# The a * b product in one piece: attention's steps and the group's issued only between products of 18 matmuls

## The chip, the cores and the metric

The kernel runs on one core of a Trainium2 chip. The time is that of one execution on the device, in microseconds. Shown for the kernel before are three runs: 725.28 us in the median, 724.61 to 728.33. TensorE (PE, and PEld for its weight loads) multiplies into PSUM, a memory of eight banks per partition; VectorE (DVE) and ScalarE (ACT) copy out of PSUM and compute element by element; GpSimd (POOL) does so in SBUF alone; SyncE (SP) issues the DMAs.

## The reference

Three layers follow one another. Attention has a sigmoid in place of the softmax; its 4 batches of 448 tokens with 12 heads of 64 make 1792 tokens of 768 values.

```python
scores = scale * np.matmul(q, k.transpose(0, 1, 3, 2)) - np.log(S)
attn_out = np.matmul(1.0 / (1.0 + np.exp(-scores)), v)
x = tokens(attn_out)                       # 1792 x 768
x = ((x @ w_a) * (x @ w_b)) @ w_out        # d_ff = 1536
logits = x @ phi                           # 8 experts x 4 slots
d = softmax over the tokens; slot_input = d.T @ x
slot_out = relu(slot_input @ w1) @ w2      # per expert
out = softmax over the slots of logits @ slot_out
```

## The kernel before, in words

The product with `w_out` is never made token by token: `w_out` is multiplied with `phi` once (`wphi`), which gives the logits from g = a * b, and the slots take their sums from g as well.

The middle of the kernel is the loop over four batches. In it, `ab` goes through the 12 chunks of 128 columns of d_ff. A chunk has two products, a (i = 0) and b (i = 1); each is 18 full matmuls of 128x128 weights with 448 columns into one "ab" PSUM buffer: weights and x are split into a high and a low part, and s = 0, 1, 2 are high*high, high*low and low*high over six pieces (L492). Behind a, ScalarE copies the result (L501), behind b, VectorE multiplies it in (L504): g^T, one of five buffers. So a batch has 24 products and 432 full matmuls. I count products from 1 in each batch.

`ab` is a generator. The loop that drives it is at the end of the listing: at each `yield` it runs `att_to`, which issues steps of attention for the next batch until their cost stands in proportion to the products done. Attention's steps are: TK and TQ, four transposes of k or q each (L147), whose results VectorE rounds into two parts (L140, L141); S, a block of six pairs of small matmuls for scores (L179), whose four results ScalarE puts through the sigmoid (L183); and PV (L193), with two results that go into the x of that batch. In batch 3, where no attention is left, the loop runs `pump`, which issues a load of the experts' weights.

Three other streams stand between the matmuls. `prep` (through `next(pr)`, three times per product) splits the weights of the next chunk; in batch 0 it also runs `beats`, which makes these weights from raw data: ScalarE converts twice (L304, L308), VectorE has three operations of about 1 us (L315, L316, L317), GpSimd adds (L322), and TensorE transposes the `w_out` pieces (L347), which ScalarE copies (L348). `group` takes four finished chunks: a sum of four small matmuls (L455; the profile counts eight), added up by ScalarE for the first group (L457) or by VectorE (L459), and then c = 0 to 3, four transposes each (L469), copied out by ScalarE and VectorE in turn (L471). `LG` does a batch's logits after its last group. `group` and `LG` are generators too; `fill_step` advances the first of them by one `yield`, and a loop on `live` forces it on when a g^T buffer is wanted that still has to be read.

L147, L347, L455, L469 and the steps of `LG` share the two PSUM buffers of the tag "ms" through batches 0 to 2; attention's S and PV have four of the tag "sc". The pool hands out a buffer as soon as its readers are issued, and TensorE then waits for these readers. All engines take their instructions in the order in which they are issued here.

Of the kernel before, what the change touches and what calls it, by code (L numbers as in the profile page):

```python
# [18 lines left out]
B, H, S, D = 4, 12, 448, 64  # L19
# [4 lines left out]
KF = FF // 128  # L24
# [9 lines left out]
def body(ctx, tc, q, k, v, w_a, w_b, w_out, phi, w1, w2, out):  # L34
# [19 lines left out]
    def ps_tile(tag, shape, bufs):  # L54
        return psp.tile(shape, F32, tag=tag, name=tag, bufs=bufs)
# [6 lines left out]
    def ms(shape=(128, S)):  # L62
        tags = banks[run["banks"]]
        tag = tags[run["ms"] % len(tags)]
        run["ms"] += 1
        return ps_tile(tag, list(shape), 4 if tag == "sc" else 2)
# [196 lines left out]
    def att_pairs(n):  # L263

        while (n - 1) not in xt:
            att_state[0] += next(att_g)
# [139 lines left out]
    def load_w(x):  # L406

        if x < 2 * NCH:
            t, i = (wr_all, x % 4) if x < LAST + 2 else (run["wr"], x % 2)
            t = t[:, i * 768:(i + 1) * 768]  # L410
            sp.dma_start(out=t, in_=ab32[x // 2 % KF, x % 2])
            w_raw[x] = t
# [10 lines left out]
    def prep(n):  # L423

        if n < KF:
            while n_split[0] <= jobs.index(("w", n, 1)):
                next(bg)
                yield
        elif 2 * n < LAST:
            for i in range(2):  # L430
                split(n, w_raw.pop(2 * n + i), dve.tensor_copy)
                for _ in range(3 if n == KF else 1):
                    next(bg, None)
                    yield
            assert next(bg, None) is None

    gT, gtok, live = {}, {}, set()
    GDEL = 2
    fill = []

    def fill_step():
        while fill:
            if next(fill[0], 0) is None:
                return
            fill.pop(0)

    def group(b, gi, evac=(act.copy, dve.tensor_copy) * 2):

        if (b, gi) != (B - 1, 2):
            for _ in range(GDEL):  # L450
                yield
        t = ms()
        for j in range(4):
            fc = 4 * gi + j
            pe.matmul(t[32 * j:32 * j + 32], wphi[:, fc], gT[b, fc], start=True, stop=True)  # L455
        if gi == 0:
            act.copy(lps, t)  # L457
        else:
            dve.tensor_tensor(lps, lps, t, op=ALU.add)  # L459
        if (b, gi) == (B - 1, 2):  # L460
            gk = e2.tile([128, 2048], F32, tag="e20", name="gk_3")
        else:
            gk = gk_01[:, gi] if gi < 2 else gk_2
        gk = gk[:T].rearrange("p (c n) -> p c n", c=C)
        yield
        for c in range(C):
            tp = ms((T, 512))
            for i in range(4):
                pe.transpose(tp[:, i * 128:(i + 1) * 128],  # L469
                             gT[b, 4 * gi + i][:, c * T:(c + 1) * T], ident)  # L470
            evac[c](gk[:, c], tp)  # L471
            yield
        for i in range(4):
            gT.pop((b, 4 * gi + i))
            live.discard(b * KF + 4 * gi + i)
        gtok[b, gi] = gk

    def ab(b):
        for fc in range(KF):
            n = b * KF + fc  # L480
            if KF <= n < LAST // 2:
                for x in (2 * n + 4, 2 * n + 5):
                    if x < LAST + 2:
                        load_w(x)
            pr = prep(n + 1)
            ws = w_sp.pop(n)
            for i in range(2):
                wh, wl = ws[i]
                t = ps_tile("ab", [128, S], 2)
                for s, (w, xi) in enumerate(((wh, 0), (wh, 1), (wl, 0))):  # L490
                    for kk in range(KD):
                        pe.matmul(t, w[:, kk * 128:(kk + 1) * 128], xt[b * NP + kk][xi],  # L492
                                  start=(s == 0 and kk == 0), stop=(s == 2 and kk == KD - 1))
                        if kk == 2:
                            yield (fc * 12 + i * 6 + s * 2 + 1) / (KF * 12)
                    if s == 2:
                        if i == 0:
                            while n - 5 in live:
                                fill_step()
                            live.add(n)  # L500
                            act.copy(gT_all[n % 5], t)  # L501
                        else:
                            g = gT_all[n % 5]
                            dve.tensor_tensor(g, g, t, op=ALU.mult)  # L504
                            gT[b, fc] = g
                            if fc % 4 == 3 and (b, fc) != (B - 1, KF - 1):
                                fill.append(group(b, fc // 4))
                    next(pr, None)
                    fill_step()
                    yield (fc * 12 + i * 6 + s * 2 + 2) / (KF * 12)  # L510
                if LAST <= 2 * n + 2 < 2 * NCH:
                    x = 2 * n + 2 + i
                    split(n + 1, w_raw.pop(x), dve.tensor_copy)
                    if x >= LAST + 2:
                        load_w(x + 2)
                    if x + 1 == 2 * NCH:
                        run.pop("wr")
                        open_slots(e1, [0])
                        pump()
            for _ in pr:  # L520
                pass
# [147 lines left out]
    def open_slots(pl, names):  # L669
        slots.extend((pl, f"{pl.name}{i}") for i in names)  # L670
# [53 lines left out]
    for b in range(B):  # L724
        if b == 1:
            cv_ctx.close()
            more_a["pool"] = ma_ctx.enter_context(tc.tile_pool(name="map", bufs=1, side="left"))
        if b == B - 1:
            ma_ctx.close()
            at_ctx.close()  # L730
            x0_ctx.close()
            e1 = ctx.enter_context(tc.tile_pool(name="e1", bufs=1, side="right"))
            run["banks"] = 1
            open_slots(e1, range(2, NE1))
            run["lsd2"] = e1.tile([128, 2048], F32, tag="e11", name="lsd2")
            run["wr"] = e1.tile([128, 2048], F32, tag="e10", name="wr")
            load_w(LAST + 2)
            load_w(LAST + 3)
        base = att_state[0]
        goal = NP * PAIR  # L740
        for i, frac in enumerate(ab(b)):
            if b < B - 1:
                att_to(base + goal * min(1.0, frac * 1.02))
            elif i % 6 == 3:
                pump()
        if b < B - 1:
            att_pairs((b + 2) * NP)
        for kk in range(NP):
            xt.pop(b * NP + kk)
        if b < B - 1:  # L750
            fill.append(LG(b))
# [18 lines left out]
    for what in order0:  # L770
        i = what[1]
        h, n, f0 = (0, 4, 4 * i) if i < 3 else (1, 6, 6 * (i - 3))
        for x in range(n):
            fc = f0 + x
# [116 lines left out]
```

## Time and profile before

| | us |
|---|---|
| median of three runs | 725.28 |
| span of the profiled execution, first to last instruction | 723.9 |
| TensorE busy in it | 681.0 |
| VectorE, ScalarE, GpSimd busy | 308.2, 272.2, 246.3 |
| batches 0, 1, 2, 3 (first to last a * b product) | 57.57 to 606.4 |

The profile's own time is its span and what lies around it; only the span is known. An end of a matmul is modelled, so starts are compared and not ends. A row of the timeline gives the start, the length, the engine, the line and what is written and read; x6 is six equal instructions in a row, and the bracket holds idle time before and what ended it.

### The profile page before, as it was taken

What the parts mean: (1) busy time and instruction counts of PE and PEld (TensorE: products, weight loads), DVE (VectorE), ACT (ScalarE), POOL (GpSimd) and SP (SyncE); (2) the same over time, 40 slices, a digit from 0 to 9 for tenths busy, and PEclk for the clock granted to TensorE, in tenths of its full rate; (3) what the DMA queues carried; (4) which work ended last, traced back from release to release, by engine and by line L of the source; (5) the groups of instructions that cost most, each with busy time, mean ns of one, the idle gap of its engine ahead of it and who ended that gap; (6) DMA issues with size and microseconds to landing.
All of it is one profiled execution on the core that took longest, in us unless ns stands there. A gap on an engine that the chain in (4) does not pass through costs nothing.

```text
span 723.9 us, 10850 instructions
## 1 busy us (share of the span) xinstructions
PE 681.0 (94%) x4231; PEld 488.4 (67%) x4231; DVE 308.2 (43%) x452; ACT 272.2 (38%) x469; POOL 246.3 (34%) x151
## 2 busy tenths in 40 slices
PE   6889998999999999999999999999999999997684
PEld 4547776777777688687776876878888896432132
DVE  3766988899843323233333232313323232300022
ACT  4888778678643414233144142330201011100021
POOL 0243766667672232232422322423344541100000
PEclk9999999999999999999999999999999999998898
DMA  9995999899971432322414322220778945999998
GB/s 213 218 267 167 280 282 287 271 289 271 297 218 42 129 101 69 117 80 80 142 53 120 101 79 63 82 67 0 276 281 322 342 160 223 380 416 416 411 351 269
DMA packets 107474, 148.99 MB, mean 206 GB/s; under 512 B 51360, under 2 KB 84384, under 8 KB 104352
## 3 DMA queue, kind: packets, MB, share of 16 engines
q1 hardware_dynamic: 107424, 148.31, 63.6%
q8 instruction: 33, 0.54, 0.3%
q14 instruction: 17, 0.14, 0.1%
HBM read 128.46 MB, written 19.83 MB: 205 GB/s over the span
## 4 chain that ended last, share of the span: by engine, by line
PE 78%; DMA 13%; DVE 3%; ACT 3%; issue 1%; SPq 0%; ACTq 0%
PE ab L492 46%; PE sc L193 10%; DMA e<-in_moe_w 9%; PE sc L179 7%; PE ms L147 3%; PE ms L469 2%; DMA wr_all<-in_moe_w_b 2%; PE ms L455 1%; ACT a L183 1%; DMA kn<-in_k 1%; PE ms L569 1%; DVE gk L317 1%; PE sc L859 1%; PE ms L347 1%; DVE gk L316 1%
## 5 line engine op out<-in xcount | busy, mean ns | idle before, releaser
L420 POOL TENSOR_TENSOR wl<-wr_all,wh 128x768 fp32r<-128x768 f32 x50 | 92.1, 1844 | 205.1 <-DVE wh L419 122.9
L492 PE MATMUL ab<-xh,wh 128*128 128x448 f32 x576 | 142.0, 376 | 0.0
L492 PE MATMUL ab<-xh,wl 128*128 128x448 f32 x576 | 141.7, 376 | 0.0
L492 PE MATMUL ab<-xl,wh 128*128 128x448 f32 x576 | 136.2, 371 | 0.0
L183 ACT ACTIVATE a<-sc,nlog 112x448 f32<-112x448 f32 x180 | 100.0, 639 | 61.8 <-PE sc L179 61.6
L492 PEld LDWEIGHTS ab<-xh,wl 128*128 128x128 f32 x576 | 104.0, 188 | 18.3 <-issue 8.6
L492 PEld LDWEIGHTS ab<-xh,wh 128*128 128x128 f32 x576 | 103.2, 188 | 19.5 <-issue 11.6
L492 PEld LDWEIGHTS ab<-xl,wh 128*128 128x128 f32 x576 | 105.9, 188 | 15.4 <-issue 7.3
L322 POOL TENSOR_TENSOR w<-gk,cy 128x768 int32<-128x768 int32 x36 | 66.2, 1838 | 93.2 <-DVE gk L317 47.0
L504 DVE TENSOR_TENSOR misc<-misc,ab 128x448 f32<-128x448 f32 x48 | 29.7, 618 | 126.2 <-PE ab L492 126.2
L501 ACT COPY misc<-ab 128x448 f32<-128x448 f32 x48 | 25.7, 536 | 153.2 <-PE ab L492 148.4
L193 PE MATMUL sc<-a,vn 112*64 112x448 f32 x384 | 76.5, 544 | 1.8 <-ACT a L183 1.8
L420 POOL TENSOR_TENSOR wl<-wr,wh 128x768 fp32r<-128x768 f32 x22 | 40.5, 1840 | 53.7 <-DVE wh L419 46.2
L193 PEld LDWEIGHTS sc<-a,vn 112*64 112x64 f32 x384 | 26.3, 136 | 43.7 <-issue 38.2
L419 DVE CAST wh<-wr_all 128x768 fp32r<-128x768 f32 x50 | 35.3, 708 | 36.8 <-POOL wl L420 22.9
L420 POOL TENSOR_TENSOR wl<-w,wh 128x768 fp32r<-128x768 f32 x24 | 45.0, 1873 | 6.5 <-ACT wh L419 6.5
L822 PE MATMUL ab<-e,gk 128*32 128x384 f32 x240 | 35.4, 559 | 11.9 <-DMA e<-in_moe_w 11.9
L179 PE MATMUL sc<-qh,kh 64*112 64x448 f32 x180 | 38.2, 415 | 1.2 <-ACT qh L140 0.6
L204 ACT ACTIVATE xh<-sc 128x448 fp32r<-128x448 f32 x24 | 13.1, 545 | 69.5 <-PE sc L193 69.4
L315 DVE TENSOR_SCALAR mf<-gk 128x768 f32<-128x768 f32 x36 | 34.1, 946 | 10.7 <-ACT gk L304 10.5
L205 DVE TENSOR_TENSOR xl<-sc,xh 128x448 fp32r<-128x448 f32 x24 | 14.9, 622 | 54.4 <-ACT xh L204 54.4
L316 DVE TENSOR_SCALAR gk<-mf 128x768 uint32<-128x768 uint32 x36 | 34.3, 953 | 1.2
(170 smaller groups left out, 727.6 us busy)
## 6 DMA issues: line engine op xcount, KB each, us to landing
e<-in_moe_w SPq DMA_DIRECT2D x23, 1024.0 KB, 8.1
wr_all<-ab SPq DMA_DIRECT2D x50, 384.0 KB, 3.3
e<-in_moe_w SPq DMA_DIRECT2D x23, 768.0 KB, 15.4
wr_cv<-in_moe_w_a SPq DMA_DIRECT2D x12, 768.0 KB, 7.1
wr_all<-in_moe_w_b SPq DMA_DIRECT2D x12, 768.0 KB, 6.7
wr_all<-in_moe_w_out SPq DMA_DIRECT2D x12, 768.0 KB, 6.8
ab<-w SPq DMA_DIRECT2D x24, 384.0 KB, 7.0
wr<-ab SPq DMA_DIRECT2D x22, 384.0 KB, 4.1
```

The costliest lines, as they stand in the source:

```text
L179: pe.matmul(sc[h], kx[r, cs], qx[r], start=(i == 0), stop=(i == 2))
L183: act.activation(a, sc[h], AF.Sigmoid, bias=nlog[:T], scale=1.0 / math.sqrt(D))
L193: pe.matmul(pv_t[g][64 * h:64 * h + 64], qkv_t["v", g][:, h, c, :], a_t.pop((g, h, c)), start=(c == 0), stop=(c == C - 1))
L315: dve.tensor_scalar(mf, m, LOW, HIGH, op0=ALU.max, op1=ALU.min)
L316: dve.tensor_scalar(mi, mf.bitcast(U32), 3, 0x3FFFFFFF, op0=ALU.logical_shift_left, op1=ALU.bitwise_and)
L322: pool.tensor_tensor(thirds(w), m.bitcast(I32), thirds(cy_t.pop(x)), op=ALU.add)
L419: rnd(wh, t)
L420: pool.tensor_tensor(wl, t, wh.bitcast(F32), op=ALU.subtract)
L492: pe.matmul(t, w[:, kk * 128:(kk + 1) * 128], xt[b * NP + kk][xi], start=(s == 0 and kk == 0), stop=(s == 2 and kk == KD - 1))
L501: act.copy(gT_all[n % 5], t)
L504: dve.tensor_tensor(g, g, t, op=ALU.mult)
L822: pe.matmul(sps[h][32 * j:32 * j + 32], hT[:, 2 * x + i, 2 * j + g], ring[order2[n + j]][0][:, i, c0:c0 + w], start=(g == 0 and x == 0 and ...
```

## The change

The generator of `ab` gives way once per product, after s = 2, and no more after each three matmuls. `fill_step` is called there alone. `group` starts one step after its last chunk and not two, the sum and c = 0 are one step, and c = 1 and 2 are one step (in batch 3's last group all stay apart). In batch 3, `pump` runs once per product as before, now behind it.

```diff
--- before.py
+++ after.py
@@ -435,7 +435,7 @@
             assert next(bg, None) is None
 
     gT, gtok, live = {}, {}, set()
-    GDEL = 2
+    GDEL = 1
     fill = []
 
     def fill_step():
@@ -462,14 +462,16 @@
         else:
             gk = gk_01[:, gi] if gi < 2 else gk_2
         gk = gk[:T].rearrange("p (c n) -> p c n", c=C)
-        yield
+        if (b, gi) == (B - 1, 2):
+            yield
         for c in range(C):
             tp = ms((T, 512))
             for i in range(4):
                 pe.transpose(tp[:, i * 128:(i + 1) * 128],
                              gT[b, 4 * gi + i][:, c * T:(c + 1) * T], ident)
             evac[c](gk[:, c], tp)
-            yield
+            if c != 1 or (b, gi) == (B - 1, 2):
+                yield
         for i in range(4):
             gT.pop((b, 4 * gi + i))
             live.discard(b * KF + 4 * gi + i)
@@ -491,8 +493,6 @@
                     for kk in range(KD):
                         pe.matmul(t, w[:, kk * 128:(kk + 1) * 128], xt[b * NP + kk][xi],
                                   start=(s == 0 and kk == 0), stop=(s == 2 and kk == KD - 1))
-                        if kk == 2:
-                            yield (fc * 12 + i * 6 + s * 2 + 1) / (KF * 12)
                     if s == 2:
                         if i == 0:
                             while n - 5 in live:
@@ -506,8 +506,9 @@
                             if fc % 4 == 3 and (b, fc) != (B - 1, KF - 1):
                                 fill.append(group(b, fc // 4))
                     next(pr, None)
-                    fill_step()
-                    yield (fc * 12 + i * 6 + s * 2 + 2) / (KF * 12)
+                    if s == 2:
+                        fill_step()
+                        yield (fc * 12 + i * 6 + 6) / (KF * 12)
                 if LAST <= 2 * n + 2 < 2 * NCH:
                     x = 2 * n + 2 + i
                     split(n + 1, w_raw.pop(x), dve.tensor_copy)
@@ -741,7 +742,7 @@
         for i, frac in enumerate(ab(b)):
             if b < B - 1:
                 att_to(base + goal * min(1.0, frac * 1.02))
-            elif i % 6 == 3:
+            else:
                 pump()
         if b < B - 1:
             att_pairs((b + 2) * NP)
```

In the order of TensorE around product 9 of batch 0 (4 chunks done, `group` of them begins; `w_` names are the recovered weights being transposed, `wl_` the low weights, `xh_` the high part of x), before:

```order
L347 MATMUL ms<-ident,w_1262 128x128 x6
L455 MATMUL ms<-misc,wphi 32x448 x4
L492 MATMUL ab<-xh_270,wl_1281 128x448
L492 MATMUL ab<-xh_370,wl_1281 128x448
L492 MATMUL ab<-xh_468,wl_1281 128x448
L147 MATMUL ms<-ident,qn 128x112 x4
L492 MATMUL ab<-xh_563,wl_1281 128x448
L492 MATMUL ab<-xh_665,wl_1281 128x448
L492 MATMUL ab<-xh_747,wl_1281 128x448
L469 MATMUL ms<-ident,misc 112x128 x4
L179 MATMUL sc<-qh,kh 112x448 x2
```

and now:

```order
L347 MATMUL ms<-ident,w_1247 128x128 x6
L494 MATMUL ab<-xh_270,wl_1281 128x448
L494 MATMUL ab<-xh_370,wl_1281 128x448
L494 MATMUL ab<-xh_468,wl_1281 128x448
L494 MATMUL ab<-xh_563,wl_1281 128x448
L494 MATMUL ab<-xh_665,wl_1281 128x448
L494 MATMUL ab<-xh_747,wl_1281 128x448
L455 MATMUL ms<-misc,wphi 32x448 x4
L470 MATMUL ms<-ident,misc 112x128 x4
L147 MATMUL ms<-ident,qn 128x112 x4
L179 MATMUL sc<-qh,kh 112x448 x2
```

The sum, the transposes of c = 0, the transposes of q and the scores' block stood at three places and now follow one another; the weights' transposes L347 keep their place. Lines from 469 on have moved by one or two.

ScalarE at the same place, before:

```order
L348 COPY wT<-ms 128x3x128 x2
L304 ACTIVATE gk_96<-wr_all 128x3x256
L308 ACTIVATE cy<-wr_all 128x768
L457 COPY misc<-ms 128x448
L501 COPY misc<-ab 128x448
L471 COPY gk_95<-ms 112x512
```

and now:

```order
L348 COPY wT<-ms 128x3x128 x2
L304 ACTIVATE gk_96<-wr_all 128x3x256
L308 ACTIVATE cy<-wr_all 128x768
L501 COPY misc<-ab 128x448
L457 COPY misc<-ms 128x448
L472 COPY gk_95<-ms 112x512
```

The copy of the sum stands behind the copy of the product.

VectorE around product 18 of batch 0, where c = 1 and 2 and the transposes of k are issued (`kh`, `kl` are the parts of k), before:

```order
L471 COPY gk_95<-ms 112x512
L315 TENSOR_SCALAR mf<-gk_96 128x768
L316 TENSOR_SCALAR gk_96<-mf 128x3x256
L317 SCALAR_TENSOR_TENSOR gk_96<-wr_cv,gk_96 128x3x256
L140 CAST kh<-ms 128x448
L141 TENSOR_TENSOR kl<-ms,kh 128x448
L504 TENSOR_TENSOR misc<-misc,ab 128x448
L471 COPY gk_95<-ms 112x512
```

and now:

```order
L315 TENSOR_SCALAR mf<-gk_96 128x768
L316 TENSOR_SCALAR gk_96<-mf 128x3x256
L317 SCALAR_TENSOR_TENSOR gk_96<-wr_cv,gk_96 128x3x256
L504 TENSOR_TENSOR misc<-misc,ab 128x448
L472 COPY gk_95<-ms 112x512
L140 CAST kh<-ms 128x448
L141 TENSOR_TENSOR kl<-ms,kh 128x448
```

The copy of c = 1 (the first copy before) stands now behind the three operations on the weights and the multiply. In the built kernel the transposes of k write into the very buffer that this copy empties.

## Rows read from the trace of the kernel before

**Rows 1.** First line of the profile's page.

```profile
span 723.9 us, 10850 instructions
```

**Rows 2.** Stretches of the batches: length, busy PE, PEld, DVE, ACT, POOL, clock, DMA share, GB/s.

```profile
57.57:214.00 156.43, 152.08 (x909) 114.78 (x908) 134.27 (x150) 116.39 (x185) 101.47 (x56) 1.00 0.87 267
214.00:357.70 143.70, 143.70 (x875) 109.37 (x874) 47.44 (x80) 43.41 (x78) 43.40 (x24) 1.00 0.33 97
357.70:501.40 143.70, 143.70 (x860) 109.94 (x859) 44.87 (x76) 43.67 (x79) 44.62 (x25) 1.00 0.25 74
501.40:606.70 105.30, 105.30 (x597) 91.72 (x595) 29.09 (x51) 13.23 (x25) 42.32 (x23) 1.00 0.70 248
```

**Rows 3.** Waits of PE in 57 to 606 us: total, times, longest.

```profile
PE ms L455 <- ACT wT L348: 2.7, 2, 2.5
PE ms L147 <- ACT wT L348: 0.8, 2, 0.5
```

**Rows 4.** Timeline of PE around one attention block: start, us, instructions.

```profile
314.55 0.77 PE L492 MATMUL ab<-xh,wl 128*128 128x448 f32 x3
...
315.54 0.36 PE L179 MATMUL sc<-qh,kl 64*112 64x448 f32 x2
...
316.65 0.87 PE L492 MATMUL ab<-xh,wl 128*128 128x448 f32 x3
317.36 1.38 PE L492 MATMUL ab<-xh,wh 128*128 128x448 f32 x6
```

**Rows 5.** Timeline of PE around four transposes.

```profile
121.40 0.60 PE L469 MATMUL ms<-ident,misc 128*112 128x128 f32 x4
121.75 1.47 PE L492 MATMUL ab<-xl,wh 128*128 128x448 f32 x6
```

**Rows 6.** Timeline of PE, first group of batch 0.

```profile
112.21 0.82 PE L347 MATMUL ms<-ident,w 128*128 128x128 f32 x6
115.54 0.96 PE L455 MATMUL ms<-misc,wphi 128*32 128x448 f32 x8 [2.51 <-ACT wT L348]
116.42 0.87 PE L492 MATMUL ab<-xh,wl 128*128 128x448 f32 x3
```

**Rows 7.** Timeline of ScalarE, first group of batch 0.

```profile
114.99 0.87 ACT L348 COPY wT<-ms 128x384 f32<-128x384 f32 x2
...
117.37 0.55 ACT L457 COPY misc<-ms 128x448 f32<-128x448 f32 x1
```

**Rows 8.** Timeline of VectorE, first group of batch 0.

```profile
122.04 0.69 DVE L471 COPY gk<-ms 112x512 f32<-112x512 f32 x1 [0.20 <-PE ms L469]
123.33 0.95 DVE L315 TENSOR_SCALAR mf<-gk 128x768 f32<-128x768 f32 x1 [0.60 <-ACT gk L304]
```

**Rows 9.** Timeline of PE, second group of batch 0.

```profile
167.99 0.82 PE L347 MATMUL ms<-ident,w 128*128 128x128 f32 x6
...
176.52 0.60 PE L469 MATMUL ms<-ident,misc 128*112 128x128 f32 x4
177.37 0.60 PE L147 MATMUL ms<-ident,kn 112*128 112x112 f32 x4 [0.25 <-DVE gk L471]
```

**Rows 10.** Timeline of ScalarE, second group of batch 0.

```profile
170.42 0.88 ACT L308 ACTIVATE cy<-wr_all 128x768 int32<-128x768 uint32 x1
```

**Rows 11.** Timeline of VectorE, second group of batch 0.

```profile
175.75 0.96 DVE L317 SCALAR_TENSOR_TENSOR gk<-wr_all,gk 128x768 uint32<-128x768 uint32 x1
176.63 0.68 DVE L471 COPY gk<-ms 112x512 f32<-112x512 f32 x1
177.23 0.94 DVE L315 TENSOR_SCALAR mf<-gk 128x768 f32<-128x768 f32 x1
...
179.19 2.21 DVE L317 SCALAR_TENSOR_TENSOR gk<-wr_cv,gk 128x768 uint32<-128x768 uint32 x1
...
182.51 0.61 DVE L504 TENSOR_TENSOR misc<-misc,ab 128x448 f32<-128x448 f32 x1
183.04 0.68 DVE L471 COPY gk<-ms 112x512 f32<-112x512 f32 x1
```


## The prediction

> **What bounds the kernel now.** I read the page first (a span of 723.9 us [rows 1]), then the stretches of the four batches, then what TensorE waits for, and last the timelines of three engines at the places where the change packs work together. In the stretches the reader is to see that TensorE has no idle time in batches 1, 2 and 3, and 156.43 - 152.08 = 4.35 us of it in batch 0 [rows 2]. VectorE and ScalarE are busy for a third of batches 1 and 2, but for 134.27 and 116.39 of the 156.43 us of batch 0 [rows 2]. So time can come only from TensorE's own instruction stream, and in batch 0 two engines with long queues stand ready to hold it up. What they hold up is a PSUM buffer: most of the 4.35 us is TensorE wanting one of the two "ms" buffers that ScalarE has not yet copied out, 2.51 us of it once [rows 3, 6]. After batch 3 comes a tail bound by loads, which starts when the last a * b product ends. I let it shift with that end.
>
> **The change, part by part.** In the order of the built kernels the products are interrupted 152 times before and 85 times now. The interrupting instructions are the same, so 67 returns to the full matmuls go, with their switches.
>
> *What a switch costs.* Full matmuls start 0.2025 us apart (six in 1.21 to 1.22). Around a lone attention block, 314.55 to 317.36 us [rows 4] hold six full matmuls (1.215) and the block: 1.595 us, of which six pairs at 0.20 are work. So 0.39 us is switching, about a quarter each on entry, after its first pair, on leaving, and on the first full matmuls after it (0.71 us for three, not 0.61). Four transposes alone take 0.35 us [rows 5], and with a tenth behind them, as in [rows 4], 0.45, or 0.11 each, which is their own pace. They switch almost for nothing, so packing transposes with anything saves little: 0.02 us a time. What saves is the end of an attention block or of a logit sum (L455) that meets transposes and not full matmuls: one slow first matmul less, 0.10 to 0.12. The order now has 11 attention blocks followed by transposes and 11 sums followed by transposes (22 x 0.11 = 2.4), and the other 45 at 0.02 make 0.9. **Sum: -3.3 us.** The bounds are 0 and 67 x 0.39 = -26, if every removed return cost what the attention block's does; the transposes' row lies near the first.
>
> *Waits that go.* The 4.35 us of batch 0 [rows 2] come where L347's two "ms" buffers are wanted again at once. Now six full matmuls (1.2 us) stand between. **-4.4 us**, and what comes back is counted next. Bounds 0 and -4.4.
>
> *Waits that come in batch 0.* There are four places: after the ninth, tenth, seventeenth and eighteenth product.
> First: L347 starts at 112.21 and takes 0.6 [rows 6]. Six full matmuls bring TensorE to 114.0. The sum needs the buffer of L348's first copy, done at about 115.4 [rows 7]: 1.4 us. The sum takes 0.88 [rows 6], four transposes 0.44, to 116.75. Then the q transposes take the sum's own buffer (so the built kernel has it). ScalarE is through its conversions at 117.37 [rows 7], and now copies a product (0.55) before it copies the sum (0.55): 118.45, so 1.7 us.
> Second: eight transposes (0.87), and the k transposes take the buffer of the first four. That copy is VectorE's. In its queue stand L315, L316, L317 and the multiply L504 ahead of it, and L315 starts at 123.3, when ScalarE delivers [rows 8]. Three at 0.97 with their gaps, 0.61 and 0.69 [rows 8, 11] make 127.5. TensorE is there at 118.45 + 1.9 (q transposes and block) + 3.65 + 0.2 + 0.87 = 125.05: 2.4 us.
> Third: L347 from 167.99 [rows 9], so TensorE at 169.8, and at 171.1 after sum and transposes. The q transposes take the buffer of the four transposes just made, whose ScalarE copy comes behind L308 (ends 171.3 [rows 10]) and a product's copy: 172.4, so 1.3 us.
> Fourth: like the second. L315 at 177.2, L316, L317, L504, copy [rows 11]; with L317 at 0.96 it ends at 181.4, with 2.21 at 182.6. TensorE is there at 172.4 + 1.9 + 3.65 + 0.2 + 0.87 = 179.0: 2.4 or 3.6. L317's two durations stand two jobs apart [rows 11]. I take the middle, 3.0. The Trainium skill, "SBUF — State Buffer", section "SBUF: two separate sides", has it that a VectorE operation with two SBUF inputs, as L317 is, and a GpSimd one lock each other out of a shared port pair for a whole instruction; with a GpSimd operation under way at 179 us, which rule and the 2.21 of [rows 11] both suggest, this wait would be 3.6 and the sum 0.6 higher.
> **Sum: 1.4 + 1.7 + 2.4 + 1.3 + 3.0 = +9.8 us.** That VectorE's queue does this shows in the kernel before: the copy L471 waited for L317, and k transposes only 0.44 us of transposes behind stood for 0.25 us [rows 9, 11]. Bounds: +2.0, if the queues are empty and each of the five is a bare copy (0.4 as worked out next), and +15, if L317 takes 2.21 everywhere and ScalarE is as late as at 111 to 115 us in all four.
>
> *Waits that come in batches 1 and 2.* The queues are short there, so only latency counts. A copy starts 0.64 us after four transposes start and takes 0.69 [rows 5, 8], so its buffer is back after 1.35 us; the next user but one arrives after 0.87: 0.5 us, once. A sum's buffer is back after about 1.7 us (0.96, a gap, 0.61), its next user arrives after 1.32: 0.4 us, twice. And twice the limit of five live product buffers forces the whole group, a sum and sixteen transposes, through two buffers at one place: 0.35 + 0.1 + 0.3 = 0.75 us each. **+2.8 us.** Bounds 0 (they fall into the switches' slack) and 5.6 (double latency).
>
> *At nothing.* Loads of q, k and v are issued up to 3.65 us later; SP then stands behind a transpose as before, and the weights of batch 0 are issued when L317 ends, which the move does not change. The logit chain after each batch takes ten products and not four, but its result is wanted at the batch after. In batch 3 the weight loads come a third of a product later. SP issues them in the same sequence as before, in which it already stood behind the small weight load. If that cover went, one load of 1 MB, some 3 us, would be late.
>
> Sum: -3.3 - 4.4 + 9.8 + 2.8 = +4.9, so a span of 728.8. The median 725.28 stands 1.4 above the profiled span, which I take as what lies around it: **730.1 us**.
>
> **The rivals.**
> (1) The queues of batch 0 let go in time. TensorE arrives later at each place than before, and if VectorE has its three operations done by then, the five waits shrink to 0.4 each, 2.0 in sum: -3.3 - 4.4 + 2.0 + 2.8 = -2.9, **722.4 us**. For it: VectorE has 22 us of idle time in batch 0 [rows 2]. Against: at 175.75 to 183.7 us its queue has no gap [rows 11]. It decides at half: with under 5 us of such waits the kernel isn't slower.
> (2) Switches cost more than I read. If packing an attention block takes half of its 0.39 away (34 of 36 blocks have neighbours now), 6.6 us more go: 723.5. For: the block's four parts [rows 4]. Against: transposes before a block spare it neither its entry nor its slow first pair.
> (3) Batch 0 becomes bound by VectorE and ScalarE: held-up transposes hold up the conversions behind them, and raw loads with them. Those waits then double, +9.8: 740. For: 134 of 156 us [rows 2]. Against: the conversions need no result of attention.
> (4) TensorE's clock falls at a wait. In batch 0 the clock reads 1.00 throughout, the 2.51 us wait included [rows 2, 6], so the 2.4 GHz level held. At the 1.2 GHz level the product behind each of the five waits would take 3.65 us more: 748. The Trainium skill, "TensorE: Matmul & The Clock Gate", section "Why this matters for your kernels", warns of idle gaps between bursts; the trace does not show it at this length.
>
> **How the numbers follow.** Forecast 0.54, rival 1 0.24, rival 2 0.13, rival 3 0.08, rival 4 0.01. 0.5% is 3.6 us, about what this kernel's measurement can tell from no change. The forecast's own range is 726 to 734, 0.7 of it above 728.9. Slower: 0.38 + 0.08 + 0.01 = 0.47. Faster: 0.10 of rival 1 (its lower part) and 0.05 of rival 2: 0.15. The same: 0.38. Range 720.5 to 736: it takes in rivals 1 and 2 but for their lowest parts, and leaves out 740 and 748.
>
> **What would show it.** The wait list of TensorE in the changed kernel should name "ms" at L147 and at L455, released by L472 and L457 or L348, some 10 to 12 us in all against 4.35. The stretch of batch 0 should be 3 to 5 us longer, batches 1 and 2 within 1 us of 143.7 each, batch 3 within 0.5 us of 105.3, the tail as long as before. The step on switches is wrong if batches 1 and 2 shorten by over 2 us each. The step on queues is wrong if batch 0 is not longer, and then the forecast falls.

## The result, and the profile after

The changed kernel takes 734.77 us in the median of six runs (732.11 to 736.56), against 727.30 for the kernel before (724.61 to 732.41): a ratio of 1.0098, with a 95% interval of 1.007 to 1.0126. It is 7.5 us slower; the forecast was 730.1, on the right side but 4.7 too low.

The first line of the page answers to [rows 1]:

```profile
span 732.4 us, 10848 instructions
```

Its own time is 734.49 us, so 2.1 us lie around the span, and not 1.4.

The stretches in [rows 2] end batches 0 to 2 some 4 us before their last product does, so that each of the next three holds a piece of the batch before it. Here they run from the first a * b matmul of a batch to that of the next one (the last to the last a * b matmul), in both kernels. First the kernel before (length, then busy PE, PEld, DVE, ACT, POOL, the granted clock, the DMA share, GB/s):

```profile
57.57:218.04 160.47, 156.12 (x937) 117.89 (x937) 134.36 (x151) 116.77 (x186) 103.00 (x56) 1.00 0.87 266
...
505.03:606.44 101.41, 101.41 (x578) 88.35 (x577) 29.09 (x51) 12.70 (x24) 42.32 (x23) 1.00 0.72 257
```

and the kernel after, in the same view:

```profile
59.10:226.40 167.30, 159.02 (x938) 120.80 (x937) 129.55 (x151) 115.62 (x186) 102.36 (x56) 0.98 0.81 255
226.40:371.90 145.50, 144.54 (x869) 111.39 (x869) 51.66 (x80) 43.87 (x78) 44.05 (x24) 1.00 0.31 93
371.90:515.30 143.40, 142.96 (x856) 110.05 (x855) 47.41 (x75) 43.97 (x79) 42.22 (x23) 1.00 0.23 71
515.30:615.90 100.60, 100.60 (x579) 88.63 (x577) 28.09 (x51) 12.88 (x24) 42.43 (x23) 1.00 0.73 259
```

Read the first two numbers of a row together: their difference is TensorE's idle time. In batch 0 it was 160.47 - 156.12 = 4.35 us and is 8.28 now, and the busy time has grown as well, from 156.12 to 159.02, with the clock at 0.98. Batches 1 and 2 have got 0.96 and 0.44 us of idle time. By the starts of single matmuls (the rows of the kernel after are cut at tenths) the batches differ by +6.8, +1.4, +0.5 and -0.95 us. The rest of the 8.5 us between the spans lies outside the loop: +1.5 ahead of it and -0.8 in the tail.

What TensorE waited for from 57 to 620 us, in the kernel after, answers to [rows 3] (total us, times, longest):

```profile
PE ms L147 <- DVE gk L472: 5.6, 3, 2.6
PE ms L147 <- ACT gk L472: 1.4, 1, 1.4
PE ms L347 <- DVE kl L141: 1.4, 1, 1.4
...
PE ms L147 <- ACT misc L457: 0.4, 1, 0.4
```

Both lines of [rows 3] are gone. In their place attention's transposes (L147) wait for the two "ms" buffers until the group's copies (L472, L457) are through.

The timeline of TensorE at the first group of batch 0, after, answers to [rows 6]:

```profile
116.31 0.96 PE L455 MATMUL ms<-misc,wphi 128*32 128x448 f32 x8
...
118.26 0.60 PE L147 MATMUL ms<-ident,qn 112*128 112x112 f32 x4 [0.42 <-ACT misc L457]
...
120.20 1.48 PE L494 MATMUL ab<-xh,wh 128*128 128x448 f32 x6
121.52 1.38 PE L494 MATMUL ab<-xl,wh 128*128 128x448 f32 x6
...
123.95 1.04 PE L470 MATMUL ms<-ident,misc 128*112 128x128 f32 x8
127.59 0.60 PE L147 MATMUL ms<-ident,kn 112*128 112x112 f32 x4 [2.60 <-DVE gk L472]
127.97 1.72 PE L494 MATMUL ab<-xh,wh 128*128 128x448 f32 x6
...
132.63 1.48 PE L494 MATMUL ab<-xh,wl 128*128 128x448 f32 x6
```

and VectorE's there answers to [rows 8]:

```profile
123.47 0.95 DVE L315 TENSOR_SCALAR mf<-gk 128x768 f32<-128x768 f32 x1 [2.32 <-ACT gk L304]
...
126.86 0.68 DVE L472 COPY gk<-ms 112x512 f32<-112x512 f32 x1
```

The copy that the k transposes need stands behind L315, L316, L317 and L504, as the prediction has it, and TensorE stands for 2.60 us. At the second group the timeline of TensorE answers to [rows 9]:

```profile
182.51 1.03 PE L470 MATMUL ms<-ident,misc 128*112 128x128 f32 x8
186.08 0.60 PE L147 MATMUL ms<-ident,kn 112*128 112x112 f32 x4 [2.53 <-DVE gk L472]
186.61 4.92 PE L193 MATMUL sc<-a,vn 112*64 112x448 f32 x16
191.46 1.49 PE L494 MATMUL ab<-xh,wh 128*128 128x448 f32 x6
...
194.58 1.46 PE L494 MATMUL ab<-xh,wl 128*128 128x448 f32 x6
```

2.53 us again. What follows both of these waits is new. Stretches of the kernel after, behind the first and behind the second of them:

```profile
129.00:132.30 3.30, 3.30 (x12) 2.87 (x11) 3.23 (x4) 0.00 (x0) 1.24 (x1) 0.50 1.02 329
187.10:190.30 3.20, 3.20 (x12) 1.17 (x10) 0.87 (x2) 0.00 (x0) 1.60 (x1) 0.50 1.00 326
```

The clock column reads 0.50, the 1.2 GHz level, behind each wait, where TensorE is busy throughout. The 16 matmuls of L193 at 186.61 take 4.92 us; the same form takes 3.23 at the full level (in a run below). Twelve full matmuls and six L347 take 132.63 - 127.97 = 4.66 us behind the first wait, and 194.58 - 191.46 = 3.12 at the full level. So the two falls cost 1.69 + 1.54 = 3.2 us. Batch 0 is then accounted for: +3.9 of idle time, +3.2 of half clock, and -0.3 for all the rest make +6.8.

These two falls belong to the execution profiled, whose granted clock over the whole span is 0.982. In the six runs it lies between 0.982 and 0.991, so not every execution loses as much to the clock; the runs at 0.989 and 0.991 took 733.00 and 732.11 us. That is 5.7 and 4.8 us above the median of the kernel before, so most of the loss does not hang on the falls.

### The profile page after: what moved, and what is told of

Same layout as the page of the kernel before. It is cut to its first block, busy times and chain, and to the rows that moved or that the text cites. A ratio compares the mean times of both kernels' runs of the same rounds, so it can differ in the third digit from the quotient of the medians.

```text
span 732.4 us, 10848 instructions
## 1 busy us (share of the span) xinstructions
PE 685.6 (94%) x4231; PEld 494.1 (67%) x4231; DVE 309.3 (42%) x452; ACT 271.9 (37%) x469; POOL 245.5 (34%) x151
## 4 chain that ended last, share of the span: by engine, by line
PE 76%; DMA 11%; DVE 6%; ACT 5%; issue 1%; SPq 0%; ACTq 0%; DVEq 0%
PE ab L494 44%; PE sc L193 10%; DMA e<-in_moe_w 9%; PE sc L179 7%; PE ms L147 3%; ACT a L183 2%; PE ms L470 2%; DVE gk L317 1%; PE ms L455 1%; PE ms L570 1%; DVE gk L316 1%; DVE mf L315 1%; DMA wr_all<-in_moe_w_b 1%; ACT gk L304 1%; PE ms L347 1%
## 5 line engine op out<-in xcount | busy, mean ns | idle before, releaser
L420 POOL TENSOR_TENSOR wl<-wr_all,wh 128x768 fp32r<-128x768 f32 x50 | 91.8, 1836 | 208.9 <-DVE wh L419 175.4
L494 PE MATMUL ab<-xh,wh 128*128 128x448 f32 x576 | 139.6, 378 | 0.0
L494 PE MATMUL ab<-xl,wh 128*128 128x448 f32 x576 | 134.2, 369 | 0.0
L494 PE MATMUL ab<-xh,wl 128*128 128x448 f32 x576 | 133.6, 367 | 0.0
L494 PEld LDWEIGHTS ab<-xh,wh 128*128 128x128 f32 x576 | 103.1, 188 | 24.5 <-issue 16.8
L494 PEld LDWEIGHTS ab<-xl,wh 128*128 128x128 f32 x576 | 108.6, 189 | 11.3 <-issue 2.5
L494 PEld LDWEIGHTS ab<-xh,wl 128*128 128x128 f32 x576 | 107.3, 188 | 8.4
L504 DVE TENSOR_TENSOR misc<-misc,ab 128x448 f32<-128x448 f32 x48 | 29.7, 619 | 129.1 <-PE ab L494 124.7
L193 PE MATMUL sc<-a,vn 112*64 112x448 f32 x384 | 79.8, 563 | 1.9 <-ACT a L183 1.8
L420 POOL TENSOR_TENSOR wl<-wr,wh 128x768 fp32r<-128x768 f32 x22 | 40.6, 1845 | 52.8 <-DVE wh L419 46.3
L193 PEld LDWEIGHTS sc<-a,vn 112*64 112x64 f32 x384 | 27.2, 142 | 45.3 <-issue 39.8
L419 DVE CAST wh<-wr_all 128x768 fp32r<-128x768 f32 x50 | 42.0, 840 | 36.8 <-issue 24.5
L420 POOL TENSOR_TENSOR wl<-w,wh 128x768 fp32r<-128x768 f32 x24 | 44.3, 1847 | 9.4 <-ACT wh L419 9.4
L823 PE MATMUL ab<-e,gk 128*32 128x384 f32 x240 | 35.7, 560 | 11.6 <-DMA e<-in_moe_w 11.5
L315 DVE TENSOR_SCALAR mf<-gk 128x768 f32<-128x768 f32 x36 | 34.0, 944 | 17.6 <-ACT gk L304 17.6
L316 DVE TENSOR_SCALAR gk<-mf 128x768 uint32<-128x768 uint32 x36 | 34.3, 953 | 1.2
L823 PEld LDWEIGHTS ab<-e,gk 128*32 128x32 f32 x240 | 10.0, 120 | 36.5 <-DMA e<-in_moe_w 24.4
```

Of the source, the lines that this page charges most:

```text
L193: pe.matmul(pv_t[g][64 * h:64 * h + 64], qkv_t["v", g][:, h, c, :], a_t.pop((g, h, c)), start=(c == 0), stop=(c == C - 1))
L315: dve.tensor_scalar(mf, m, LOW, HIGH, op0=ALU.max, op1=ALU.min)
L316: dve.tensor_scalar(mi, mf.bitcast(U32), 3, 0x3FFFFFFF, op0=ALU.logical_shift_left, op1=ALU.bitwise_and)
L419: rnd(wh, t)
L420: pool.tensor_tensor(wl, t, wh.bitcast(F32), op=ALU.subtract)
L823: pe.matmul(sps[h][32 * j:32 * j + 32], hT[:, 2 * x + i, 2 * j + g], ring[order2[n + j]][0][:, i, c0:c0 + w], start=(g == 0 and x == 0 and ...
```

## The experiments

The first four were made on one chip and timed against 23 runs of the kernel before (727.23 us), the others against 27 (727.50).

**Attention alone between products.** The group and `fill_step` stay as before. Against the kernel before:

```diff
-                        if kk == 2:
-                            yield (fc * 12 + i * 6 + s * 2 + 1) / (KF * 12)
...
                     next(pr, None)
                     fill_step()
-                    yield (fc * 12 + i * 6 + s * 2 + 2) / (KF * 12)
+                    if s == 2:
+                        yield (fc * 12 + i * 6 + 6) / (KF * 12)
...
-            elif i % 6 == 3:
+            else:
                 pump()
```

> Theory A (three "ms" results packed into one place must wait for a copy that stands in VectorE's or ScalarE's queue; behind the two longest waits TensorE's clock falls): with attention's steps at product ends alone and the group's steps at thirds of a product as before, a copy again has six matmuls of time, so batch 0 has 4 to 6 us of waits and no clock fall: +0 to +2 us against the kernel before (0 to +0.3%). Theory B (packing attention's steps costs by itself, whatever stands beside them): most of the change's +7 us stays, +5 to +7. Theory C (batch 0 is bound by VectorE and ScalarE, and any packing shifts their work): +3 to +7, with batch 0 longer by that.

Measured: 725.49 us, ratio 0.9976 (0.9963 to 0.9988), 1.7 us faster, so somewhat better than the 0 to +2 us of theory A. Batch 0 takes 158.87 us, 1.6 less than before. What TensorE waits for in 57 to 620 us of this run begins so:

```profile
PE ms L455 <- ACT wT L348: 2.0, 2, 1.7
PE ms L347 <- DVE kl L141: 1.7, 2, 1.4
```

None of the waits of L147 for the group's copies is there, and no stretch at half clock in the four batches. So attention's packing costs nothing by itself over the whole kernel, which rules out theory B; the loss needs the group's part. In batches 1 and 2 it does cost something: they take 144.46 and 143.23 us, 0.4 and 0.3 more than before.

**The group alone between products.** The other half of the change. Against the kernel after, attention's two yields and `pump` are put back:

```diff
+                        if kk == 2:
+                            yield (fc * 12 + i * 6 + s * 2 + 1) / (KF * 12)
...
                     if s == 2:
                         fill_step()
-                        yield (fc * 12 + i * 6 + 6) / (KF * 12)
+                    yield (fc * 12 + i * 6 + s * 2 + 2) / (KF * 12)
...
-            else:
+            elif i % 6 == 3:
                 pump()
```

> The group packed at product ends, attention at sixths of a product as before. Theory A: the k and q transposes stand three or more matmuls away from the group's in batch 0, which halves the waits at the four places: +0 to +3 us against the kernel before. Theory B: attention is as before, so -2 to +1. Theory C: +3 to +7, batch 0 longer.

Measured: 738.69 us, 1.0152 (1.0129 to 1.0175): 11.5 us slower, worse than both parts together, and outside what my theory allowed. Batch 0 takes 170.74 us. TensorE's timeline at its second group:

```profile
188.60 1.07 PE L470 MATMUL ms<-ident,misc 128*112 128x128 f32 x4 [3.19 <-DVE kl L141]
```

c = 1 and c = 2, packed, want both buffers at once. One of them still held k's transposes, made in the middle of the product, and VectorE had not done their casts (L141): 3.19 us of idle time, and two such waits, 2.69 us and this one, make 5.9 of the list; the clock falls at both. The stretch from 188.20 to 194.80, which begins just before the wait ends, is at 0.50 for its whole length:

```profile
188.20:194.80 6.60, 6.20 (x18) 2.40 (x20) 1.38 (x3) 0.59 (x1) 2.87 (x2) 0.50 0.72 214
```

So the costly part is the group's, and what holds it up depends on which step of attention took a buffer shortly before. Packing attention as well makes the change cheaper, not dearer.

**Copies ahead of the conversions.** Against the kernel after, the step of `prep` at a product's end in batch 0 (behind b also the one before it) is issued only after the group's and attention's steps, so that their copies stand first in the queues:

```diff
-                    next(pr, None)
+                    if b or s == 0 or (s, i) == (1, 0):
+                        next(pr, None)
                     if s == 2:
                         fill_step()
                         yield (fc * 12 + i * 6 + 6) / (KF * 12)
+                        if b == 0:
+                            for _ in range(1 + i):
+                                next(pr, None)
```

> The changed kernel with the same packing; in batch 0 alone the conversions of the weights are issued behind the group's and attention's steps of a product end and not ahead of them, so that the copies no longer stand behind L315 to L317. Theory A: the waits of batch 0 fall from 9.6 us to 3 to 5, no clock fall in it: batch 0 8 us shorter than in the changed kernel, and the whole -1 to +2 us against the kernel before. Theory B: packing is the same, so +5 to +7. Theory C: the conversions are later and the work of VectorE the same, so +6 to +10.

Measured: 733.03 us, 1.0083 (1.0059 to 1.0107). Batch 0 takes 165.56, only 1.7 less than in the kernel after. From the list of TensorE's waits, 57 to 620 us:

```profile
PE ms L347 <- DVE wphi L373: 3.0, 3, 1.3
PE ab L494 <- POOL wl L420: 1.7, 3, 0.9
PE ms L147 <- DVE gk L472: 1.5, 3, 0.5
PE ms L147 <- ACT misc L457: 1.3, 1, 1.3
```

The waits for VectorE's L472 fall from 5.6 to 1.5 us and no stretch of batch 0 is at half clock: that much of theory A holds. The time that it forecast, -1 to +2 us, did not come. The measured +5.8 us is what theory B forecast, and nearly what C did. As causes of the change's loss both are ruled out by the run with attention alone, which they had slower; but C's words on the later conversions fit this run, since these now hold up something else. L347 waits 3.0 us for an "ms" buffer, because L373, the copy that empties it, has come to stand behind L315 to L317 in VectorE's queue. The products themselves (L494) wait 1.7 us for `wl`, the low weights, which come late. So this run shows that the waits for the group's copies come from the order in VectorE's queue, and that turning the order round moves the waiting elsewhere.

**Batch 0 as before, the rest changed.** Against the kernel after:

```diff
-            for _ in range(GDEL):
+            for _ in range(2 if b == 0 and gi < 2 else 1):
...
-        if (b, gi) == (B - 1, 2):
+        if (b, gi) == (B - 1, 2) or (b == 0 and gi < 2):
...
-            if c != 1 or (b, gi) == (B - 1, 2):
+            if c != 1 or (b, gi) == (B - 1, 2) or (b == 0 and gi < 2):
...
+                        if kk == 2 and b == 0:
+                            yield (fc * 12 + i * 6 + s * 2 + 1) / (KF * 12)
...
-                    if s == 2:
+                    if s == 2 or b == 0:
                         fill_step()
-                        yield (fc * 12 + i * 6 + 6) / (KF * 12)
+                        yield (fc * 12 + i * 6 + s * 2 + 2) / (KF * 12)
```

> The changed kernel with batch 0 issued as in the kernel before. Theories A and C: what the change costs lies in batch 0, so +0 to +2 us against the kernel before (batch 1 +1.4, batch 2 +0.5, batch 3 -0.9 in the changed kernel's profile). Theory B: batches 1 and 2 are packed too and hold two thirds of the attention: +3 to +5.

Measured: 728.97 us, 1.0026 (1.0005 to 1.0047): 1.7 us slower, as theories A and C had it and not B. Batch 0 takes 161.27; the others 145.54, 143.65 and 100.45, as in the kernel after. So some 5.7 of the 7.5 us are batch 0's. This run also holds a surprise. It has the order of [rows 6], and the same L455 waits for the same copy, 1.81 us. On TensorE's timeline:

```profile
116.30 1.70 PE L455 MATMUL ms<-misc,wphi 128*32 128x448 f32 x8 [1.81 <-ACT wT L348]
```

The stretch that follows, with the clock as in the rows above:

```profile
116.50:119.70 3.20, 3.20 (x14) 1.54 (x7) 1.35 (x1) 2.17 (x4) 2.15 (x2) 0.50 0.87 292
```

It is at 0.50. In the profiled execution of before, 2.51 us at this place were followed by 1.00 [rows 2, 6]. So the length of such a wait does not settle by itself whether the clock falls behind it.

**The wait filled.** Is it that TensorE stands still? Against the kernel after, 12 matmuls stand between the transposes of c = 1, 2 and those of k in the tenth and eighteenth product of batch 0; they write to the next product's buffer, which that product's first matmul overwrites, and add work and no result.

```diff
+        nxt = []
...
-                t = ps_tile("ab", [128, S], 2)
+                t = nxt.pop() if nxt else ps_tile("ab", [128, S], 2)
...
+                        if b == 0 and i == 1 and fc in (4, 8):
+                            nxt.append(ps_tile("ab", [128, S], 2))
+                            for _ in range(12):
+                                pe.matmul(nxt[0], w[:, :128], xt[b * NP][0], start=True, stop=True)
```

> The changed kernel, with twelve additional full matmuls (2.4 us, their result is overwritten) in batch 0 at the tenth and eighteenth product's end, between the group's eight transposes and the k transposes that wait there for 2.7 us. Theory D (TensorE's clock falls behind these waits because it stands still in them): the waits shrink to 0.1 to 0.4 us, no half clock at 129 and 187 us, batch 0 163.5 to 164.5 and not 167.3 us: 3 us below the changed kernel, some +4 against the kernel before. Rival (the clock falls on its own at times, as it does once in the first 57 us of most profiles): batch 0 167 to 168, +7.

Measured: 731.77 us, 1.0057 (1.0034 to 1.008), 3.0 less than the kernel after. Batch 0 takes 164.44. Its second group on TensorE's timeline:

```profile
182.38 2.67 PE L515 MATMUL ab<-xh,wl 128*128 128x448 f32 x12
185.13 0.60 PE L147 MATMUL ms<-ident,kn 112*128 112x112 f32 x4
185.66 3.23 PE L193 MATMUL sc<-a,vn 112*64 112x448 f32 x16
```

and the two stretches that were at 0.50:

```profile
187.10:190.30 3.20, 3.20 (x17) 1.83 (x14) 0.76 (x2) 0.55 (x1) 0.67 (x1) 1.00 1.05 314
129.00:132.30 3.30, 3.30 (x21) 3.06 (x20) 3.20 (x5) 1.10 (x3) 1.48 (x1) 1.00 0.97 326
```

Both are at 1.00, and L193 takes 3.23 us. The copy is as late as it was, since L147 starts 2.75 us after the filling began; the extra matmuls only lie in the time of the wait. Batch 0 is 2.9 us shorter than in the profiled execution of the kernel after, as theory D had it, which agrees with the 3.2 of the rows. This is one profiled execution of each kernel; but the six runs here have a granted clock of 0.986 to 0.989, and three of the six of the kernel after have 0.982 or 0.983. So it is likely, though not certain, that the two falls come from the standing still and not by chance.

**Attention packed where it is free, the group packed only late.** From here on the edits are made on the kernel before. `late_g` names the groups that are packed: the last of batch 2 and the first two of batch 3, which are issued in batch 3, where no attention is left.

```diff
+    def late_g(b, gi):
+        return (b, gi) in ((B - 2, 2), (B - 1, 0), (B - 1, 1))
...
-            for _ in range(GDEL):
+            for _ in range(1 if late_g(b, gi) else GDEL):
...
-        yield
+        if not late_g(b, gi):
+            yield
...
-            yield
+            if c != 1 or not late_g(b, gi):
+                yield
...
-                        if kk == 2:
+                        if kk == 2 and not (b < B - 1):
...
-                    fill_step()
-                    yield (fc * 12 + i * 6 + s * 2 + 2) / (KF * 12)
+                    if s == 2 or b < B - 1:
+                        fill_step()
+                    if s == 2 or not (b < B - 1):
+                        yield (fc * 12 + i * 6 + s * 2 + 2) / (KF * 12)
```

> Attention's steps at product ends in all batches, the group's packed at product ends in batch 3 alone (with the last group of batch 2, which runs there), elsewhere at thirds. Theory A2 (packing the group costs wherever attention's transposes share its two buffers, and saves switches where they don't; packing attention alone costs nothing): batch 0 as with attention alone (158.9 us), batch 3 100.45 and not 101.4, so 0.9 below the run with attention packed alone: about -2.6 us against the kernel before. Rival (the shorter batch 3 belongs to the later logits of the packed batches 1 and 2, not to its own group): batch 3 stays at 101.4, -1.7 us.

Measured: 724.99 us, 0.9971 (0.995 to 0.9993). It is 2.5 us faster, as theory A2 had it: batch 3 takes 100.45 instead of 101.41, batch 0 158.59. The rival, by which batch 3 stays at 101.4, is out.

**The same with attention packed in batch 0 alone** (called e6 further on; `b == 0` for both `b < B - 1` that guard the yields):

> As the run before it, but attention at product ends in batch 0 alone, at sixths in batches 1 and 2. Theory A2 with the stretches of the runs so far: batch 0 158.9, batches 1 and 2 144.1 and 142.9 as in the kernel before (not 144.5 and 143.2), batch 3 100.45: -2.5 us or, if those 0.7 us of batches 1 and 2 come on top, 0.7 below the run before it. Rival: packed attention saves in every batch, so this is slower than the run before it by 0.5 or more.

Measured: 724.13 us, 0.995 (0.993 to 0.9971): 3.4 us faster than the kernel before by the medians, the best of all, though not to be told from the last one by its interval. So its rival, that attention's packing saves in every batch, did not come. Its batches 0 and 3:

```profile
58.03:216.17 158.14, 155.33 (x937) 119.09 (x937) 128.63 (x151) 115.86 (x186) 102.38 (x56) 1.00 0.86 270
...
503.20:603.70 100.50, 100.50 (x579) 88.65 (x577) 27.43 (x51) 12.89 (x24) 42.41 (x23) 1.00 0.73 258
```

Idle time in batch 0 is 158.14 - 155.33 = 2.81 us against 4.35, and busy time 155.33 against 156.12. Batch 0 gives 2.3 us and batch 3 1.0; batches 1 and 2 stay at 144.11 and 142.91, as before.

**And with the groups of batch 0 one step later** (`GDEL` of 3 there):

```diff
-            for _ in range(1 if late_g(b, gi) else GDEL):
+            for _ in range(1 if late_g(b, gi) else 3 if b == 0 else GDEL):
```

> As e6, with the groups of batch 0 begun one third of a product later, so that the logit sum stands six full matmuls behind L347 and not right behind it. Theory A2: the 2.0 us that L455 waits there for ScalarE's copies shrink to 0.5: batch 0 157.4, 1.4 us below e6, about -4 us against the kernel before. Rival (the sum now stands together with q's transposes and the attention block at one product end, and its buffer is wanted again at once): a wait of L147 for L457 or L459 takes its place, batch 0 158.5 to 159.5, as e6.

Measured: 727.74 us, 0.9999 (0.998 to 1.0018); batch 0 takes 161.71. The rival was right that a new wait takes the place of the old one, but it named the sum's copy and at most 159.5 us. The list of waits has a new first line, for the copies of the group's transposes (L475 in this run):

```profile
PE ms L147 <- DVE gk L475: 2.5, 2, 1.6
```

So attention's transposes meet the group's copies again. One third of a product is worth 3.6 us here.

## Why the prediction was right, and where it was not

**Place and mechanism: right.** Batch 0 is longer, because attention's transposes want "ms" buffers that the group's copies still hold, and the copies stand in VectorE's queue behind L315 to L317 and L504. The runs show it from three sides: without the group's packing these waits are absent (attention alone), with batch 0 as before most of the loss is gone, and with the copies first in the queue these waits shrink, though others take their place. Of the signs that were named, L147 is in the list as forecast, with 7.8 us in all and not 10 to 12; L455 is not in it. Batch 0 is 6.8 us longer and not 3 to 5, and batch 3 is 0.95 shorter, which is outside the 0.5 that was given.

**The new waits of batch 0: +9.8 predicted, +8.3 measured.** The second, third and fourth place came as priced: 2.4, 1.3 and 3.0 predicted, 2.60, 1.4 and 2.53 measured. The fourth took the lower of the two ends, since L317 took 0.96 us. By the port rule of the Trainium skill, "SBUF — State Buffer", section "SBUF: two separate sides", it would have been 3.6 with a GpSimd operation under way. None is: one has ended at 183.04 us, and the next starts at 185.12, after L317 is through.

```profile
181.19 1.85 POOL L420 TENSOR_TENSOR wl<-w,wh 128x768 fp32r<-128x768 f32 x1 [0.63 <-ACT wh L419]
...
183.93 0.96 DVE L317 SCALAR_TENSOR_TENSOR gk<-wr_cv,gk 128x768 uint32<-128x768 uint32 x1
...
185.12 1.81 POOL L322 TENSOR_TENSOR w<-gk,cy 128x768 int32<-128x768 int32 x1 [2.08 <-ACT cy L308]
```

So the trace agrees with the rule; what the prediction could not tell is which job would meet a GpSimd operation.

The first place was priced at 1.4 + 1.7 and cost 0.42. The step had taken over from [rows 6, 7] that L348 copies 2.8 us after L347 starts. Here it is 0.5 us (L347 at 114.33), and L455 waits for nothing. ScalarE in the kernel after:

```profile
114.86 0.86 ACT L348 COPY wT<-ms 128x384 f32<-128x384 f32 x2 [0.19 <-PE ms L347]
```

ScalarE's lateness in the kernel before came from a load. Its L304 had stood for raw weights there:

```profile
111.30 0.91 ACT L304 ACTIVATE gk<-wr_all 128x768 f32<-128x768 f32 x1 [2.48 <-DMA wr_all<-in_moe_w_b]
```

In the run with batch 0 as before, the same L304 waits 1.88 us for the same load, so it was not that one execution's. In the kernel after it waits for nothing at this place, and TensorE comes to L347 2.1 us later; the prediction had let ScalarE keep its times while the order moved. One wait had not been foreseen: the weights' transposes stood behind the casts of k. TensorE around it:

```profile
95.14 0.37 PE L179 MATMUL sc<-ql,kh 64*112 64x448 f32 x2
95.44 0.60 PE L147 MATMUL ms<-ident,kn 112*128 112x112 f32 x4
95.81 1.46 PE L494 MATMUL ab<-xh,wh 128*128 128x448 f32 x6
97.11 1.38 PE L494 MATMUL ab<-xl,wh 128*128 128x448 f32 x6
...
100.17 0.52 PE L347 MATMUL ms<-ident,w 128*128 128x128 f32 x3 [1.35 <-DVE kl L141]
```

That L347 waited 1.35 us for k's cast (L141), which VectorE came to after L315 to L317. So 0.42 + 2.60 + 1.4 + 2.53 + 1.35 make the 8.3. That the sum came so near is in part luck: the first place was priced 2.7 us too high, and the 1.35 was not in the sum.

**Switches: -3.3 predicted, about -1.7 by an estimate from the rows.** This is the mis-sized term. The rows just shown have the end of a scores' block that meets transposes: 0.30 us to the transposes, where pairs follow each other at 0.20, so leaving the block costs its 0.10 there too, and the six full matmuls behind the transposes take 97.11 - 95.81 = 1.30, not 1.215. Behind a block without transposes they take 121.52 - 120.20 = 1.32. Both kinds of neighbour leave a slow first matmul; a meeting saves one of two, and 0.02 goes back to the four transposes (0.37, not 0.35). All places of a kind can be compared by the time from the last full matmul before them to the third one behind, less 0.2025 for each of the three. A scores' block alone takes 1.60 us, four transposes of q or k 0.41, and the two in a row 1.95: 0.06 is saved and not 0.11. A sum alone takes 1.09, four transposes of the group 0.44, and the two in a row 1.48: 0.05. Eight transposes in a row take 0.87, which saves 0.01. So 22 x 0.055 + 45 x 0.01 = 1.7.

**Batches 1 and 2: +1.9 in sum.** Their waits were priced at +2.8 and took 1.40 us of visible idle time. The rest is latency that no bracket shows: over the whole loop the interruptions, idle time and half clock left out, take 193.0 us by the reckoning just given and 193.3 before, so only 0.3 us less and not 1.7. The difference of 1.4 would be that latency, which makes the 2.8 right in sum, though the rows do not part it by batches. Batch 1 came out 1.4 us longer, just outside the 1 us that was given.

**The clock: given 1 in 100 and 18 us, came in part, 3.2 us.** The step "the clock held 1.00 through the 2.51 us wait" was one execution. In the kernel after the falls follow the two longest waits only, and each costs 1.5 to 1.7 us, not the 3.65 that were priced. The Trainium skill, "TensorE: Matmul & The Clock Gate", section "Why this matters for your kernels", warns of idle gaps between bursts, but of longer ones. Behind 2.53, 2.60 and 2.69 us, and once behind 1.81, the traces show a fall, and behind the 2.51 of [rows 6] they show none, so here the measurements decide.

**The sum.** Against the forecast's span of 728.8 the profiled one has +3.2 (clock), +1.6 (switches), -1.5 (waits of batch 0), -0.7 (the pace of full matmuls in batch 3, below), +1.5 (ahead of the loop) and -0.8 (tail), with the waits of batches 1 and 2 as priced. That is 3.3 of the 3.6 us up to 732.4; 0.3 stay open. The 0.7 us more around the span, the 0.3 between the profiled run and the median, and 0.1 of rounding in the forecast (725.28 + 4.9 is 730.2) make the rest of the 4.7. The kernel before has itself a median of 727.30 in six runs, not 725.28, so the rise is 7.5 us against the 4.9 that were forecast. The 734.77 lies within the stated 720.5 to 736, but outside the 726 to 734 of the forecast alone: without the 3.2 of the clock, a share of rival 4, to which 0.01 was given, it would lie in both.

## What to carry to other kernels

Steps that each need a buffer pair and a copy on a queue with other work should not be packed into one gap: the spread of three matmuls between them was what hid the copies. Pack what leaves its results elsewhere or finds the buffers free (attention alone in batch 0 here, or the group after attention has ended), and look first at which queue the copy stands in. A wait on TensorE like those of 1.8 to 2.6 us here may cost more than its length, since the clock can drop to half behind it.

## What the runs showed of the hardware that was not expected

Full matmuls of 448 columns follow each other at one of two distances, and keep to it for long runs. In batch 3 of the kernel before, six start in 1.24 us:

```profile
540.85 1.40 PE L492 MATMUL ab<-xh,wl 128*128 128x448 f32 x6
542.09 1.40 PE L492 MATMUL ab<-xh,wh 128*128 128x448 f32 x6
```

and in that of the kernel after in 1.22:

```profile
556.85 1.38 PE L494 MATMUL ab<-xl,wh 128*128 128x448 f32 x6
558.07 1.38 PE L494 MATMUL ab<-xh,wl 128*128 128x448 f32 x6
```

In batch 3 of the kernel before 183 of the distances lie in such runs at 206 to 207 ns, and in that of the kernel after none; the others are near 202.5. At 4 ns each, about 0.7 of the 0.95 us that batch 3 gained is this. The run with attention alone, whose batch 3 is issued as before, has the 183 again, and the seven runs with the group packed in batch 3 have none. So there the distance goes with the order of the instructions and not with the execution; what in the order chooses it is open.

L317 has its two durations from GpSimd. Of the 36 in the kernel before and the 36 in the kernel after, 18 each take 0.96 us. The 18 others of each, up to 2.55 and 2.15 us long, all start while a GpSimd operation runs, and end 0.81 to 0.82 us behind its end. The 2.21 us of [rows 11] is one of them: a GpSimd operation (L420) ran there from 178.74 to 180.59 us.

The clock also falls once in the first 57 us in most of the executions profiled, at about 24 or 47 us, though the program is the same there in all of them (after: from 47.1 us; before: not at all). The stretch ahead of the loop is then 59.1 to 60.4 us long, and 57.6 to 58.0 otherwise: this is the +1.5 above. As the program is the same up to there, I don't count it as an effect of the change.
